# A state-space transform's last two pointwise operations on GpSimd, their input in two buffers, and kernel loads on SyncE's queue

## The chip, the cores and the metric

The kernel runs on one core of one Trainium2 chip. The time is the device time of one execution in microseconds (us), lower is better. The engines are named as in the profile: PE is TensorE's matmul, DVE is VectorE, ACT is ScalarE, POOL is GpSimd, and SP is SyncE, which here only issues DMAs.

## The reference

Two independent computations stand side by side in the output. Part A is a memory-augmented recurrent transformer, 64 segments one after the other. Part B is a long convolution of the S4 kind, and the change lies in it:

```python
P = jnp.exp(logdA[:, :, None] * l[None, None, :])
K = jnp.einsum('dn,dnl,dn->dl', Cc, P, dB).real
Kf = rfft2(pad(K)); Uf = rfft2(pad(u.transpose(0, 2, 1)))
Yf = Uf * Kf[None, :, :, :]
y = irfft2(Yf)[..., :L].transpose(0, 2, 1) + u * Dskip
return jnp.concatenate([a, b], axis=-1)
```

Here L is 2048, the model has 1024 channels, and all inputs and the output are bf16.

## The kernel before, in words

The program runs part B first, then part A. Part A needs weights that are loaded once (residents) and weights that are streamed again in each of the 64 segments.

Part B first builds the convolution kernel K and the spectra of u; K goes to DRAM as Kd, the spectra of u go there as Ud. What follows is the transform, from about 508 us of the profiled execution to 807 us. The channels are cut in two halves, dh=0 and dh=1, of 512 channels (DH). For each dh there are four frequency blocks kc, and each block is done in two half blocks, half=0 and half=1. One half block is one pass of the loop in `pointwise`:

- PE multiplies the kernel values KT with the cosine and sine matrix MF (L1137): 32 matmuls into two PSUM tiles s_[0] and s_[1]. There are three such PSUM buffers.
- ACT copies s_[1] into o_ (L1142, or L1144 and L1145).
- DVE adds and subtracts: X1 and X2 (L1150, L1151). Each reads s_[0] from PSUM and o_ from SBUF.
- DVE multiplies with the spectra of u: M1 to M4 (L1157 and L1158, twice each). They read uq and x, both in SBUF, in f32.
- DVE subtracts and adds in Y: Y1 and Y2 (L1159, L1160), both inputs in SBUF.
- DVE adds and subtracts the two halves of Y into Bt, as bf16 (L1163, twice): the last two operations of the half block.
- In dh=1, `inverses(2)` follows: two output blocks of dh=0 are made by 16 matmuls each (L1209), ACT scales the result into yb (L1214), DVE multiplies uu by Dskip and adds yb (L1215, L1216), and GpSimd issues the DMA that stores it (L1217).

Each engine runs its own instructions in program order, so an instruction that waits holds up all that follow on its engine. The same holds for the queues that issue DMAs. SP's queue in the transform holds, in this order for each frequency block: the loads mi and uu of the inverses (`load_inverse`, L1172 and L1174, three blocks ahead; uu has four buffers, freed when the store of a result has landed), and then the four loads uq of the next block's spectra (`load_u`, L963; four buffers, freed by M1 to M4). GpSimd's queue holds the 31 loads KT of the kernel values of dh=1 (`load_k`, L936, issued after the first block of dh=0), and the stores of the inverses. `load_k` for dh=0 runs earlier and on SP. The tile y has one buffer, x and o_ have one each.

After the eight half blocks of dh=1 come the remaining 16 inverses, those of dh=1, which read all of the second Bt. Beside each of them ACT issues two loads of part A's resident weights (L193). Then part A runs.

Of the kernel before, what the change touches and what calls it, by code (L numbers as in the profile page):

```python
# [10 lines left out]
BF16 = mybir.dt.bfloat16  # L11
F32 = mybir.dt.float32
# [584 lines left out]
def part_b(ctx, tc, u, A_re, A_im, B_re, B_im, C_re, C_im, log_dt, Dskip, out_b, ahead, copies, residents):  # L597
# [5 lines left out]
    DH, DQ = 512, 256  # L603
    v, sc, gp, pe, sy = nc.vector, nc.scalar, nc.gpsimd, nc.tensor, nc.sync
# [323 lines left out]
    def load_k(dh, qs, KT):  # L928
        dsl = slice(DH * dh, DH * dh + DH)

        def rows(r0, n, step=1):
            return Kd[r0:r0 + step * (n - 1) + 1:step, dsl]
        n_q = [0]

        def get(out, in_):
            qs[n_q[0] % len(qs)].dma_start(out=out, in_=in_)  # L936
            n_q[0] += 1
        for r in (0, 2, 1, 3):
            k0 = KT[:, 4 * r, :]
            get(k0[0:64], rows(r, 64, 4))  # L940
            get(k0[64:128], rows(256 + (0, 0, 1, 2)[r], 64, 2))
            k1 = KT[:, 4 * r + 1, :]
            if r == 2:
                get(k1[0:128:2], rows(384, 64, 2))
                get(k1[1:128:2], rows(386, 64, 2))
            else:
                get(k1[:], rows(384 + (0, 0, 0, 1)[r], 128))
            for mc in (2, 3):
                k2 = KT[:, 4 * r + mc, :]
                q0 = 512 + 64 * (mc - 2)  # L950
                get(k2[0:128:2], rows(q0, 64))
                if r == 0:
                    get(k2[1:128:4], rows(q0, 32, 2))
                    get(k2[3:128:4], rows(q0 + 2, 32, 2))
                else:
                    get(k2[1:128:2], rows(q0 + 1, 64))
        return KT

    def load_u(dh, kc):
        us = {}  # L960
        for q in (0, 2, 1, 3):
            us[q] = ahead.pool.tile([128, 2, 2, DQ], F32, name="uq", tag="wsl", bufs=4)
            sy.dma_start(out=us[q][:].rearrange("p a c d -> p a (c d)"), in_=Ud[kc, 2 * dh:2 * dh + 2, :, q].rearrange("a p c d -> p a (c d)"))  # L963
        return us
# [109 lines left out]
    for f in range(-1, 17):  # L1074
        if f == 15:
# [4 lines left out]
            ks = [load_k(0, (sy,), ahead.pool.tile([128, 16, DH], BF16, name="KT", tag="kst"))]  # L1080
# [32 lines left out]
    ktp = ctx2.enter_context(tc.tile_pool(name="b_KT", bufs=1))  # L1113
    bp0 = ctx2.enter_context(tc.tile_pool(name="b_B0", bufs=1))
    pw = ctx2.enter_context(tc.tile_pool(name="b_pw", bufs=1))
# [5 lines left out]
    def negate(KT):  # L1121
        KN = ahead.pool.tile([128, 8, DH], BF16, name="KN", tag="xTl")
        sc.activation(out=KN[:], in_=KT[:, 8:16, :], func=ACT.Copy, scale=-1.0)
        return KN

    def pointwise(dh, kc, KT, Bt):
        us = spectra.pop(0)
        for half in range(2):

            s_ = []  # L1130
            for r in range(2):
                ps = ps_h.tile([128, 2, DH], F32, name="hps", tag="h")
                for cs in range(2):
                    for i, rr in enumerate((r, r + 2)):
                        for mc in range(4):
                            rhs = KNs[dh][:, 4 * (rr - 2) + mc, :] if half == 1 and i == 1 else KT[:, 4 * rr + mc, :]
                            pe.matmul(ps[:, cs, :], lhsT=MF[:, 4 * rr + mc, cs, 128 * kc:128 * kc + 128], rhs=rhs,  # L1137
                                      start=(i == 0 and mc == 0), stop=(i == 1 and mc == 3))
                s_.append(ps)
            o_ = pw.tile([128, 2, DH], F32, name="osb_", tag="o")  # L1140
            if half == 0:
                sc.copy(out=o_[:], in_=s_[1][:])  # L1142
            else:
                sc.copy(out=o_[:, 0, :], in_=s_[1][:, 1, :])  # L1144
                sc.activation(out=o_[:, 1, :], in_=s_[1][:, 0, :], func=ACT.Copy, scale=-1.0)  # L1145
            if len(KNs) == dh:
                KNs.append(negate(KT))
            qs = (0, 2) if half == 0 else (3, 1)
            X = pw.tile([128, 2, 2, DH], F32, name="x", tag="x")
            v.tensor_tensor(out=X[:, 0], in0=s_[0][:], in1=o_[:], op=ALU.add)  # L1150
            v.tensor_tensor(out=X[:, 1], in0=s_[0][:], in1=o_[:], op=ALU.subtract)  # L1151
            Y = pw.tile([128, 2, 2, DH], F32, name="y", tag="y")
            split = "p c (a d) -> p c a d"
            for n_, q in enumerate(qs):
                uc, un = (us[q][:, :, i, :].unsqueeze(1).to_broadcast([128, 2, 2, DQ]) for i in range(2))
                x_ = X[:, n_].rearrange(split, a=2)
                v.tensor_tensor(out=Y[:, n_].rearrange(split, a=2), in0=uc, in1=x_, op=ALU.mult)  # L1157
                v.tensor_tensor(out=x_, in0=un, in1=x_, op=ALU.mult)  # L1158
            v.tensor_tensor(out=Y[:, :, 0, :], in0=Y[:, :, 0, :], in1=X[:, :, 1, :], op=ALU.subtract)  # L1159
            v.tensor_tensor(out=Y[:, :, 1, :], in0=Y[:, :, 1, :], in1=X[:, :, 0, :], op=ALU.add)  # L1160
            first = 0 if half == 0 else 1
            for j, op in ((0, ALU.add), (1, ALU.subtract)):
                v.tensor_tensor(out=Bt[:, kc, half, j], in0=Y[:, first], in1=Y[:, 1 - first], op=op)  # L1163
            inverses(2 if dh == 1 else 0)

    NIV = 3
# [1 line left out]
    def load_inverse(dh, c):  # L1168
        r, mc = c // 4, c % 4
        iv = ivs[-1]  # L1170
        mi = iv.tile([128, 2, 4, 128], BF16, name="mi", tag="mi", bufs=NIV)
        sy.dma_start(out=mi[:], in_=MId[c])  # L1172
        uu = iv.tile([128, 512], BF16, name="uu", tag="uu", bufs=NIV + 1)
        sy.dma_start(out=uu[:], in_=u_v[r, mc][:, DH * dh:DH * dh + DH])  # L1174
        return mi, uu
# [11 lines left out]
    def inverses(n):  # L1187

        for _ in range(n):
            dh_, c = todo.pop(0)  # L1190
            if not ready:
                ready.append(negated(c, nxt[0][0]))
            inverse(dh_, Bs[dh_], c, *nxt.pop(0), *ready.pop(0))
            if len(todo) >= NIV:
                nxt.append(load_inverse(*todo[NIV - 1]))
# [26 lines left out]
    for dh in range(2):  # L1222
        Bt = (bp0, bp)[dh].tile([128, 4, 2, 2, 2, DH], BF16, name="Bt", tag="B")
        Bs.append(Bt)
        if dh == 1:

            resident = residents()
            next(resident)
            todo = [(0, c) for c in range(16)] + [(1, c) for c in range(16)]
            nxt = [load_inverse(*todo[n_]) for n_ in range(NIV)]  # L1230
        for kc in range(4):
            pointwise(dh, kc, ks[dh], Bt)
            if kc < 3 or dh == 0:
                spectra.append(load_u(dh + (kc + 1) // 4, (kc + 1) % 4))
            if dh == 0 and kc == 0:
                ks.append(load_k(1, (gp,), ktp.tile([128, 16, DH], BF16, name="KT", tag="KT")))
    ctx2.close()
    ctx_m.close()
    for c in range(16):
# [4 lines left out]
def kernel(  # L1244
# [53 lines left out]
    with ExitStack() as ctx_b:  # L1298
        part_b(ctx_b, tc, B_u[0], B_A_re, B_A_im, B_B_re, B_B_im, B_C_re, B_C_im, B_log_dt, B_Dskip, out_b, ahead, copies, residents)
# [37 lines left out]
```

## Time and profile before

| what | us |
|---|---|
| median of 4 runs | 2485.24 |
| lowest and highest run | 2477.5, 2498.34 |
| the profiled execution's own time | 2477.5 |
| its span, first to last instruction | 2475.8 |
| L1163, one of the two last operations, on DVE, f32 to bf16, 1024 elements in each of 128 partitions | 1.22 |
| L1217, issue of a store on GpSimd | 0.54 |
| L936, issue of a KT load: on SP (median), on GpSimd (median) | 0.594, 0.542 |

The whole page's first lines give the shares over the span:

```profile
PE 2013.3 (81%) x32728; PEld 1082.0 (44%) x32774; DVE 1471.2 (59%) x3159; ACT 964.8 (39%) x1543; POOL 352.0 (14%) x629
PE   1689888866988688888888888888888888888879
DVE  9589788979881254545454545454545454545540
POOL 2235556540001100000000000000000000000020
DMA  6685964664349999999999999999999999999992
```

The first line gives each engine's busy time, its share of the span and its number of instructions. The others cut the span in 40 slices of 61.9 us; a digit is the busy share of a slice in tenths. The transform lies in slices 8 to 12, counted from 0. In slices 8 to 11 DVE has digits 7, 9, 8 and 8, GpSimd 4, 0, 0 and 0. A line of a timeline gives the start, the duration, engine, line, operation, output and inputs with their shapes, the number of instructions merged in it, and in brackets the idle time before it and what ended it. [...]

### The profile page before, as it was taken

The page shows a single profiled execution, that of the slowest core. Times are in us where ns is not written, and L with a number is a line of the kernel's source. Part 1 is how long each engine was busy: PE and PEld are TensorE (multiplying, and loading weights), DVE is VectorE, ACT ScalarE, POOL GpSimd, SP SyncE. Part 2 cuts the span into 40 slices and gives each one's busy share as a digit, 9 for nine tenths or more (in the row PEclk, how much of TensorE's full clock was granted, in tenths as well). Part 3 has the DMA queues.
Part 4 walks back from the last instruction along what each step waited for, and adds up shares of the span by engine and source line. Part 5 has one row for each costly group of instructions (what it writes and reads, how often), then busy time and mean ns, then how long its engine had stood idle before and what let it go on. Part 6 is the DMA issues. An engine that isn't in the chain of part 4 may idle for free.

```text
span 2475.8 us, 76297 instructions
## 1 busy us (share of the span) xinstructions
PE 2013.3 (81%) x32728; PEld 1082.0 (44%) x32774; DVE 1471.2 (59%) x3159; ACT 964.8 (39%) x1543; POOL 352.0 (14%) x629
## 2 busy tenths in 40 slices
PE   1689888866988688888888888888888888888879
PEld 1355565632433244444444444444444444444444
DVE  9589788979881254545454545454545454545540
ACT  6689788911212132323232333232333333333321
POOL 2235556540001100000000000000000000000020
PEclk9999999987989799999999999999999999999999
DMA  6685964664349999999999999999999999999992
GB/s 160 182 230 156 268 185 142 161 180 138 104 152 348 341 384 389 373 370 376 380 381 383 364 394 387 371 366 385 377 389 382 386 382 373 379 381 388 384 384 77
DMA packets 383273, 763.17 MB, mean 308 GB/s; under 512 B 119462, under 2 KB 211590, under 8 KB 380886
## 3 DMA queue, kind: packets, MB, share of 16 engines
q1 hardware_dynamic: 363094, 700.46, 78.4%
q0 software_dynamic: 14928, 39.99, 5.0%
q10 hardware_dynamic: 4912, 17.84, 2.0%
q8 instruction: 256, 4.19, 0.7%
q14 instruction: 83, 0.68, 0.1%
HBM read 703.35 MB, written 67.88 MB: 312 GB/s over the span
## 4 chain that ended last, share of the span: by engine, by line
DMA 32%; PE 29%; DVE 18%; issue 13%; ACT 6%; POOL 1%; SPq 1%; DVEq 0%; ACTq 0%; POOLq 0%
DMA wst<-WD_k 15%; PE acc L339 11%; DMA wst<-WD_o 9%; PE pp L438 3%; PE pe L561 2%; PE pro L158 2%; DVE nr L1026 2%; DMA wst<-WD_v 2%; PE ups L848 2%; PE tr L350 2%; DMA PVd<-vst 1%; DVE piece L278 1%; PE pa L995 1%; DMA wst<-WD_q 1%; DVE sc L385 1%
## 5 line engine op out<-in xcount | busy, mean ns | idle before, releaser
L339 PEld LDWEIGHTS <-hT 128*32 128x32 bf16 x12352 | 325.9, 96 | 466.2 <-issue 248.1
L339 PE MATMUL acc<-wst,hT 128*32 128x512 bf16 x3072 | 311.6, 390 | 161.3 <-DMA wst<-WD_k 66.0
L345 ACT CAST ev<-acc 128x512 bf16<-128x512 f32 x384 | 224.7, 585 | 406.0 <-PE acc L339 401.5
L438 PEld LDWEIGHTS <-oT 128*32 128x32 bf16 x8192 | 204.0, 97 | 111.5 <-issue 84.6
L278 DVE TENSOR_SCALAR piece<-keep 128x256 int32<-128x256 int32 (+1 forms) x640 | 191.5, 363 | 57.8 <-PE pp L438 31.2
L438 PE MATMUL pp<-W_o,oT 128*32 128x256 bf16 x5120 | 211.7, 276 | 8.1 <-DMA W_o<-in_A_Wo_dram 8.1
L339 PE MATMUL acc<-W_v,hT 128*32 128x512 bf16 x3072 | 210.9, 379 | 0.0
L377 DVE TENSOR_REDUCE mx<-sc 128x8 f32<-128x320 f32 x128 | 62.3, 487 | 243.4 <-PE sc L370 243.3
L339 PE MATMUL acc<-W,hT 128*32 128x512 bf16 x2560 | 204.4, 390 | 0.0
L351 DVE COPY KT<-tr 128x512 bf16<-128x512 bf16 x64 | 27.2, 425 | 261.8 <-PE tr L350 261.8
L438 PE MATMUL pp<-wst,oT 128*32 128x256 bf16 x2560 | 128.9, 278 | 33.4 <-DMA wst<-WD_o 24.3
L358 POOL COPY KT<-pk 128x128 bf16<-128x128 bf16 x128 | 37.7, 294 | 794.5 <-PE sc L370 447.3
L351 ACT COPY QT<-tr 128x512 bf16<-128x512 bf16 x128 | 74.9, 586 | 189.0 <-PE tr L350 189.0
L1209 PE MATMUL yp<-Bt,mi 128*128 128x512 bf16 x379 | 113.4, 405 | 35.1 <-DMA mi<-MId 27.3
L425 ACT CAST oT<-pv 128x512 bf16<-128x512 f32 x128 | 75.0, 586 | 170.4 <-PE pv L411 166.0
L339 PE MATMUL acc<-W_q,hT 128*32 128x512 bf16 x1792 | 134.2, 380 | 0.0
L312 POOL COPY hT<-xt 128x192 bf16<-128x192 bf16 x64 | 22.2, 347 | 729.5 <-DMA xt<-XTd 518.8
L158 PE MATMUL pro<-xTl,wsl 128*128 128x512 bf16 x493 | 120.7, 392 | 6.0 <-ACT xTl L102 5.2
L379 ACT ACTIVATE sc<-sc 128x320 f32<-128x320 f32 x128 | 54.0, 422 | 154.3 <-DVE sc L378 148.7
L339 PE MATMUL acc<-W_k,hT 128*32 128x512 bf16 x1536 | 107.3, 385 | 0.0
L1137 PE MATMUL hps<-KT,MF 128*128 128x512 bf16 x374 | 94.3, 397 | 15.9 <-DVE x L1151 14.9
L350 PE MATMUL tr<-a_ident,ev 128*128 128x128 bf16 x1024 | 101.7, 222 | 1.0 <-ACT KT L351 1.0
(280 smaller groups left out, 3627.0 us busy)
## 6 DMA issues: line engine op xcount, KB each, us to landing
wst<-WD_o SPq DMA_DIRECT2D x320, 512.0 KB
wst<-WD_k SPq DMA_DIRECT2D x256, 512.0 KB
wst<-WD_q SPq DMA_DIRECT2D x256, 512.0 KB
wst<-WD_v SPq DMA_DIRECT2D x256, 512.0 KB
Ud<-ux POOLq DMA_DIRECT2D x16, 1024.0 KB, 5.7
uq<-Ud SPq DMA_DIRECT2D x32, 512.0 KB
pk<-PKd SPq DMA_DIRECT2D x64, 192.0 KB
wsl<-in_A_Wk_dram SPq DMA_DIRECT2D x16, 512.0 KB
```

Of the source, the lines that this page charges most:

```text
L158: nc.tensor.matmul(a[:], lhsT=w[:, kc, 128 * j:128 * j + 128], rhs=xTl[:, kc, :, :].rearrange("p s k -> p (s k)"), start=(kc == 0), stop=( ...
L278: nc.vector.tensor_scalar(out=out.bitcast(I32), in0=in_.bitcast(I32), scalar1=0, scalar2=None, op0=ALU.bitwise_or)
L339: nc.tensor.matmul(a[32 * g:32 * g + 32, o_:o_ + rhs.shape[1]], lhsT=hT[:, kc, :], rhs=rhs, start=(kc == 0), stop=(kc == KC - 1), tile_pos ...
L345: nc.scalar.copy(out=q[:], in_=a[:])
L350: nc.tensor.transpose(out=p[:, i, hl, :, :].rearrange("p a b -> p (a b)"), in_=q[:, 128 * hl:128 * hl + 128], identity=ident[:])
L351: eng(out=dst, in_=p[:, i, :, :, :])
L377: nc.vector.tensor_reduce(out=mx[:], in_=sc, axis=AX.X, op=ALU.max)
L379: nc.scalar.activation(out=sc, in_=sc, func=ACT.Exp, scale=scale)
L425: nc.scalar.copy(out=o[:], in_=p[:].rearrange("p a (g q) -> p a g q", g=4))
L438: nc.tensor.matmul(po[32 * qt:32 * qt + 32, :], lhsT=oT[:, h % 4, (h % 16) // 4, :], rhs=columns(w, 1024 * hh + 256 * qt, 256)[0][1], star ...
L1137: pe.matmul(ps[:, cs, :], lhsT=MF[:, 4 * rr + mc, cs, 128 * kc:128 * kc + 128], rhs=rhs, start=(i == 0 and mc == 0), stop=(i == 1 and mc = ...
L1209: pe.matmul(yp[:], lhsT=m_[:, cs, kc, :], rhs=Bt[:, kc, half, j, c_, :], start=(n == 0), stop=(n == 15))
```

## The change

It has three parts, all in the transform of part B.

```diff
-            Y = pw.tile([128, 2, 2, DH], F32, name="y", tag="y")
+            Y = pw.tile([128, 2, 2, DH], F32, name="y", tag="y", bufs=2)
...
             first = 0 if half == 0 else 1
             for j, op in ((0, ALU.add), (1, ALU.subtract)):
-                v.tensor_tensor(out=Bt[:, kc, half, j], in0=Y[:, first], in1=Y[:, 1 - first], op=op)
+                (v if (dh, kc, half) == (1, 3, 1) else gp).tensor_tensor(out=Bt[:, kc, half, j], in0=Y[:, first], in1=Y[:, 1 - first], op=op)
...
             if dh == 0 and kc == 0:
-                ks.append(load_k(1, (gp,), ktp.tile([128, 16, DH], BF16, name="KT", tag="KT")))
+                ks.append(load_k(1, (sy,), ktp.tile([128, 16, DH], BF16, name="KT", tag="KT")))
```

The two operations that write Bt go from DVE to GpSimd in 15 of the 16 half blocks; in the very last one they stay on DVE. Their input y has two buffers instead of one. The 31 loads of the kernel values for dh=1 are issued by SP instead of GpSimd, at the same place in the program, so in SP's queue they stand behind the uq loads of block kc=1 and ahead of those of kc=2.

## The prediction

> **What bounds the kernel now.** I read the page first. Its second part puts the change, which touches only part B's transform, into slices 8 to 11 of 40; from slice 12 on the DMA engines are nine tenths busy. Next I asked for busy time in stretches: 518 to 614 us holds the eight half blocks of dh=0, 614 to 745 those of dh=1, and after that come the last inverses and part A.
>
> ```profile
> core 0: us, PE busy (x) PEld busy (x) DVE busy (x) ACT busy (x) POOL busy (x), PEclk, DMA share, GB/s
> 518.00:614.00 96.00, 62.57 (x247) 26.18 (x251) 93.92 (x81) 15.70 (x15) 19.30 (x36) 0.86 0.45 142
> 630.00:745.00 115.00, 102.97 (x449) 45.47 (x457) 94.57 (x102) 24.84 (x39) 8.59 (x16) 0.94 0.42 136
> 745.00:809.00 64.00, 51.32 (x211) 21.52 (x213) 11.19 (x28) 17.28 (x26) 10.16 (x34) 0.92 0.96 343
> 870.00:1000.00 130.00, 111.76 (x2308) 59.04 (x2300) 72.40 (x199) 42.01 (x82) 4.68 (x15) 1.00 1.02 386
> ```
>
> DVE is busy 93.9 of 96 us in dh=0, so DVE is the bound there. In dh=1 neither PE nor DVE is full. From 745 us the DMA share is 0.96 and more: weights stream in, and they start only when the transform ends. So what DVE gains or loses before its last Bt write moves the end of the kernel one for one. The view of waits for 620 to 745 us agrees: PE yp waits 7.3 us for DVE Bt.
>
> Then the DVE timeline, one half block of dh=0 (Y2, the two operations that move, X1 and X2 of the next half, its first multiplication M1):
>
> ```profile
> 551.08 1.22 DVE L1160 TENSOR_TENSOR y<-y,x 128x1024 f32<-128x1024 f32 x1
> 552.33 2.36 DVE L1163 TENSOR_TENSOR Bt<-y 128x1024 bf16<-128x1024 f32 x2
> 554.61 1.22 DVE L1150 TENSOR_TENSOR x<-hps,osb__7370 128x1024 f32<-128x1024 f32 x1
> 555.74 1.22 DVE L1151 TENSOR_TENSOR x<-hps,osb__7370 128x1024 f32<-128x1024 f32 x1
> 556.88 1.22 DVE L1157 TENSOR_TENSOR y<-uq,x 128x1024 f32<-128x1024 f32 x1
> ```
>
> One half runs from 542.77 to 554.61, 11.84 us, of which the pair takes 2.28 (552.33 to 554.61). In dh=1 the four short uu operations (U1 to U4) follow the pair, and at every second half DVE waits for uq:
>
> ```profile
> 639.38 1.22 DVE L1160 TENSOR_TENSOR y<-y,x 128x1024 f32<-128x1024 f32 x1
> 640.63 2.36 DVE L1163 TENSOR_TENSOR Bt<-y 128x1024 bf16<-128x1024 f32 x2
> 643.43 0.42 DVE L1216 TENSOR_TENSOR uu<-uu,yb 128x512 bf16<-128x512 bf16 x1
> 644.15 0.54 POOL L1217 DMA_DIRECT2D out_dram<-uu  x1 [15.84 <-DVE uu L1216]
> 646.25 0.33 SPq L1174 DMA_DIRECT2D uu<-in_B_u_dram  x1
> 646.63 3.30 SPq L963 DMA_DIRECT2D uq<-Ud  x4
> 652.23 1.23 DVE L1157 TENSOR_TENSOR y<-uq,x 128x1024 f32<-128x1024 f32 x1 [5.07 <-DMA uq<-Ud]
> ```
>
> The reader is to see a chain: U2 ends, GpSimd issues the output's DMA, its landing frees a uu buffer, SP (in order) loads uu and only then uq, and M1 starts 12.85 us after Y2 started.
>
> **What the Trainium skill says.** "SBUF — State Buffer", section "Who interferes with whom": VectorE and GpSimd share a port pair. A VectorE instruction with two SBUF inputs contends with a GpSimd instruction that reads SBUF, and the one that comes second "fully blocks" until the first is done; with at most one SBUF input, outside the two-port modes, it does not. The trace agrees wherever it can. These rows carry it:
>
> ```profile
> L864 POOL TENSOR_TENSOR ux<-us x16: 1262/1268/1277, 115.6 to 491.4; 128x512 f32<-128x512 f32 x16
> L867 POOL TENSOR_TENSOR ux<-us x64: 717/1222/1614, 118.1 to 496.9; 128x256 f32<-128x256 f32 x64
> L977 DVE TENSOR_TENSOR gi<-E,sn x32: 1106/1112/1647, 122.7 to 503.2; 128x1824 bf16<-128x1824 bf16 x32
> L860 DVE TENSOR_TENSOR us<-ua,ups x32: 675/680/682, 109.6 to 491.2; 128x512 f32<-128x512 f32 x32
> ```
>
> L860 reads one operand from PSUM; sixteen of its executions lie beside the GpSimd sum of L864, and neither stretches. L867 takes 0.72 us alone and up to 1.61 where VectorE runs L1026 and L1033 beside it. The one L977 that starts within an L867 (497.82) takes 1.65 instead of 1.11. That is one sighting for two SBUF inputs, in bf16; for f32 none.
> "GPSIMD Engine Reference", section "Performance versus the Vector engine", prices a two-input f32 sum of 2048 elements at 4497 ns, and the trace has 512 at 1268 ns. A line through both gives an estimate of 2.34 us for 1024; twice the 1.235 between two starts of L864 and L865 gives 2.47. I take 2.4.
>
> **The change part by part.** Call the moved pair P1 and P2, the multiplications M1 to M4, and s the start of Y2.
>
> (1) *The pair leaves DVE*: 15 of 16 halves, 2.28 us each. X1 and X2 read one operand from PSUM, so they run beside P1. M1 to M4, Y1, Y2 and U1 to U4 read two from SBUF and take turns with P1 and P2.
>
> (2) *A half of dh=0 after the change.* Y2 ends at s+1.22; GpSimd follows 0.1 later (L864 starts 0.08 to 0.2 after its DVE input), P1 from s+1.32 to s+3.72. X1 starts at s+1.14, M1 would start at s+3.41 and waits until 3.72. P2 is queued behind M1: M1 ends at 4.85, P2 at 7.25, and M2 waits for that. M2 to the next Y2 is 4.80 (546.28 to 551.08), so the next Y2 is at s+12.05 instead of 11.84: 0.2 worse. The first pair is hidden, since DVE waits there for ACT anyway (530.92, idle 0.68). Seven periods: +1.5 us. The gain is eaten almost exactly. Bounds of a period: -0.1 with P at 2.25, +0.5 with 2.55.
>
> (3) *An even half of dh=1.* U1 comes before P1 and holds to s+1.50; P1 to 3.90, U2 to 4.25, P2 to 6.65; only then U3, and 1.02 later X1 (643.78 to 644.80), at s+7.67. X1 to M1 is 2.27, M1 to Y2 6.05 (652.23 to 658.28): s+15.99, where before the step is 13.57 (658.28 to 671.85). +2.4. Here nothing free of the shared port lies beside P1 and P2.
>
> (4) *A half that waits for uq.* The output's DMA is behind P2 in GpSimd's queue and is issued at s+6.75, not s+4.77. Landing, uu, uq and M1 move with it: M1 at about s+14.85, while DVE is ready at s+9.94. +2.0.
> In dh=1 the first half absorbs its pair in the 3.59 us for which DVE waits for ACT (631.06), and the last stays on DVE. There remain three of each: 3*(2.4+2.0) = +13.2 us.
>
> (5) *Y in two buffers*: without it M1 of the next half would wait for P2. With it the buffer is free a half earlier; costs nothing.
>
> (6) *Kernel loads to SP.* The 31 KT DMAs leave GpSimd, where they ran from 526.9 to 547 and would have held P1 back. On SP they come after the uq of kc=1 (last at 538.09) and take about 21.5 us, as the first 31 did there (469.52). So the next uq goes out near 560 instead of 547.5 and is needed at 568.7: 8.7 us of room against 5.6 from issue to use above, so nothing lost; without this cover up to 3. KT is wanted at 592.5. "DMA: Bandwidth & Descriptors", section "Issuing engines are not separate DMA queues", says that the transfers run on the same 16 engines whoever issues, so I expect no speed from the move itself.
>
> Sum: 1.5+13.2, about +15 us. Against the profiled execution (2477.5 us, span 2475.8) that is 2492.5. The median of the runs shown is 7.7 higher, 2485.24, so I forecast 2500.
>
> **The rivals.**
> A, the forecast: whole instructions exclude each other. P between 2.25 and 2.55 gives +11 to +19, 2496 to 2504; the runs shown lie up to 13 us from their median, of which I allow 6 on either side: 2490 to 2510.
> B, partial: the f32 operations lose only about half of this, by waits that DVE has anyway. Between A and C: about -5 us, 2480. For it: DVE idles for uq in any case. Against it: that idle time lies after the pair, not beside it.
> C, the other side: f32 operations at one element per cycle leave the shared read path open. Then DVE gains 2.28 in seven halves (-16), gives back some 3 where uq(kc=2), issued at 560, is wanted at 561.9, and in dh=1 the output's DMA goes out 2.28 earlier: periods 16.6 and 11.3, sum 83.7 instead of 95.6 (639.38 to 734.94), -12. Together -25: 2460. For it: no f32 pair was seen side by side. Against it: L977, which reads through the same two inputs. It decides if M2 is not stretched. With a wait of w for each of P1 and P2, A's sum is about 7*(w-2.28)+3*(2w-2.4)+3*(2w-2.8) while P1 fits beside X1 and X2; it changes its sign at w = 1.7 us, below the lowest estimate of P.
> D, worse: SP's longer queue also costs uq transfers in dh=0, or a late output delays the mi loads and so PE: 10 to 20 more, about 2513.
>
> **How the numbers follow.** A 0.60, B 0.10, C 0.20, D 0.10. A measurement of this kernel tells about 0.5%, 12.4 us, from nothing; A straddles that bound, and some six tenths of it lie above. Slower: 0.37+0.10, rounded to 0.48; same: 0.23+0.10, less rounding 0.31; faster 0.21. The range 2474 to 2516 takes in A, B and most of D and leaves C out. A's own range is 2490 to 2510.
>
> **What would show it.** Steps 1 and 2: P rows of about 2.4 us on POOL and, in dh=0, X rows still 1.22 while M1 and M2 read above 1.22, the one or the other by some 2 us; the period near 12. Step 3: U2 and U3 near 2.5 us instead of 0.42. Step 4: the first output DMA of a half some 6.7 us after Y2 starts. Step 6: uq at about 560 with no DVE wait behind it. A period of 9.6 in dh=0 would prove me wrong, and so would Bt's last write before 735 us.

## The result and the profile after

| | before | after |
|---|---|---|
| median of the runs, us | 2488.65 (64 runs) | 2495.25 (43 runs) |
| lowest and highest, us | 2477.5, 2514.28 | 2480.72, 2512.33 |
| the profiled execution, us | 2477.5 | 2489.41 |
| its span, us | 2475.8 | 2487.7 |

The ratio after to before is 1.0026 with a 95% interval of 1.0015 to 1.0037. Taken times 2488.65 that is 6.5 us slower, between 3.7 and 9.2. Single runs scatter by more than that; only the many runs side by side show it.

First the stretches of the span that the prediction read, now for the kernel after:

```profile
core 0: us, PE busy (x) PEld busy (x) DVE busy (x) ACT busy (x) POOL busy (x), PEclk, DMA share, GB/s
518.00:614.00 96.00, 62.47 (x249) 26.21 (x254) 91.33 (x67) 15.08 (x14) 40.39 (x19) 0.85 0.44 145
630.00:745.00 115.00, 96.86 (x416) 42.44 (x424) 99.65 (x81) 23.20 (x36) 35.98 (x24) 0.92 0.38 125
745.00:809.00 64.00, 52.54 (x207) 21.83 (x210) 14.63 (x33) 15.54 (x23) 8.09 (x15) 0.88 0.89 314
```

From 518 to 614 us DVE ran 67 instructions instead of 81 and was still busy 91.33 us instead of 93.92. The 14 fewer would have freed 14 times 1.14 (half of the pair's 2.28), 16 us. So most of what left came back as longer rows: an instruction that waits for GpSimd in its row counts as busy. From 630 to 745 us DVE was *busier*, 99.65 against 94.57, with 21 instructions fewer. These two windows don't hold the same work, though: before, the last Bt write ended at 738.55, and after, the window closes before the last one.

The timeline shows where. Two halves of dh=0, one after the other, on DVE and GpSimd (a DVE row can start some 0.1 us before the row ahead of it ends, as 552.74 after 551.60 plus 1.23, so a period is taken from start to start):

```profile
538.57 1.22 DVE L1160 TENSOR_TENSOR y<-y,x 128x1024 f32<-128x1024 f32 x1
539.87 5.72 POOL L1163 TENSOR_TENSOR Bt<-y 128x1024 bf16<-128x1024 f32 x2 [7.74 <-DVE y L1160]
542.17 1.22 DVE L1157 TENSOR_TENSOR y<-uq,x 128x1024 f32<-128x1024 f32 x1
543.42 3.26 DVE L1158 TENSOR_TENSOR x<-uq,x 128x1024 f32<-128x1024 f32 x1
...
550.25 1.22 DVE L1160 TENSOR_TENSOR y<-y,x 128x1024 f32<-128x1024 f32 x1
551.54 4.65 POOL L1163 TENSOR_TENSOR Bt<-y 128x1024 bf16<-128x1024 f32 x2 [5.95 <-DVE y L1160]
551.60 1.23 DVE L1150 TENSOR_TENSOR x<-hps,osb__7370 128x1024 f32<-128x1024 f32 x1
552.74 1.22 DVE L1151 TENSOR_TENSOR x<-hps,osb__7370 128x1024 f32<-128x1024 f32 x1
553.87 3.41 DVE L1157 TENSOR_TENSOR y<-uq,x 128x1024 f32<-128x1024 f32 x1
557.31 1.23 DVE L1158 TENSOR_TENSOR x<-uq,x 128x1024 f32<-128x1024 f32 x1
...
562.11 1.22 DVE L1160 TENSOR_TENSOR y<-y,x 128x1024 f32<-128x1024 f32 x1
```

X1 and X2 (L1150, L1151), which read one operand from PSUM, keep their 1.22 us with GpSimd's pair beside them. A multiplication with both inputs in SBUF does not: in the first half M2 waits (3.26), in the second M1 (3.41). From Y2 to Y2 these halves take 11.68 and 11.86 us; before it was 11.84.

In dh=1, from the Y2 of a half that waits for uq:

```profile
638.61 1.22 DVE L1160 TENSOR_TENSOR y<-y,x 128x1024 f32<-128x1024 f32 x1
639.91 4.96 POOL L1163 TENSOR_TENSOR Bt<-y 128x1024 bf16<-128x1024 f32 x2 [10.81 <-DVE y L1160]
640.26 2.40 DVE L1216 TENSOR_TENSOR uu<-uu,yb 128x512 bf16<-128x512 bf16 x1
642.58 2.57 DVE L1215 TENSOR_TENSOR uu<-uu,Dsk 128x512 bf16<-128x512 bf16 x1
644.82 0.56 POOL L1217 DMA_DIRECT2D out_dram<-uu  x1
645.60 1.22 DVE L1150 TENSOR_TENSOR x<-hps,osb__7868 128x1024 f32<-128x1024 f32 x1
648.41 0.33 SPq L1174 DMA_DIRECT2D uu<-in_B_u_dram  x1
648.80 1.96 SPq L963 DMA_DIRECT2D uq<-Ud  x4
653.12 1.23 DVE L1157 TENSOR_TENSOR y<-uq,x 128x1024 f32<-128x1024 f32 x1 [5.18 <-DMA uq<-Ud]
```

U2 and U3 take 2.40 and 2.57 us instead of 0.42. The store, whose data U2 wrote by 642.66, is issued 2.2 us later, when GpSimd's pair has ended. M1 starts 14.51 us after Y2 (before: 12.85).

The view of waits from 620 to 745 us (engine, line, what it waited for: us in total, times, longest) gives DVE's largest:

```profile
DVE y L1157 <- DMA uq<-Ud: 13.1, 3, 5.2
```

It was 13.3 us, also three times. The longer halves did not use up this wait: it comes after the pair, and what ends it, the uq transfer, was itself made late.

The Y2-to-Y2 steps of dh=1, us, from the timelines. s0 is the first half of dh=1 and s7 the last; the last column runs from the first X1 to the end of the last write of Bt.

| | first X1 to s0 | s0 to s7 | the seven steps of dh=1 | to last Bt |
|---|---|---|---|---|
| before | 103.82 | 112.81 | 17.25, 18.90, 13.57, 17.56, 13.57, 18.03, 13.92 | 220.24 |
| after | 103.14 | 122.88 | 17.77, 20.58, 15.30, 19.37, 15.29, 19.29, 15.28 | 229.63 |

dh=0 gained 0.7 us and dh=1 lost 10.1, so the transform was 9.4 us longer in these two executions.

The first step of dh=1 is not set by the pair. X1 of its second half waits for ACT, ACT for PE's matmuls L1137, which come behind those of the inverses L1209 on PE, and these had waited for mi, the load of the first inverse. Before:

```profile
614.41 8.55 PE L1209 MATMUL yp<-Bt,mi 128*128 128x512 bf16 x31 [14.81 <-DMA mi<-MId]
631.06 1.23 DVE L1150 TENSOR_TENSOR x<-hps,osb__7757 128x1024 f32<-128x1024 f32 x1 [3.59 <-ACT osb__7757 L1145]
```

After:

```profile
630.29 1.23 DVE L1150 TENSOR_TENSOR x<-hps,osb__7757 128x1024 f32<-128x1024 f32 x1 [2.03 <-ACT osb__7757 L1145]
```

Counted from the transform's first X1 (518.31 and 517.70), this X1 stands at 112.75 before and at 112.59 after. So most of the 0.7 us that dh=0 gained is gone at this point, the step reads 0.5 longer because it starts earlier, and the pair of this half costs nothing.

### The profile page after: what moved, and what is told of

It reads as the page before. It is cut to its first block, busy times and chain, and to the rows that moved or that the text cites. A ratio compares the mean times of both kernels' runs of the same rounds, so it can differ in the third digit from the quotient of the medians.

```text
span 2487.7 us, 76294 instructions
## 1 busy us (share of the span) xinstructions
PE 2017.2 (81%) x32728; PEld 1080.5 (43%) x32774; DVE 1480.5 (60%) x3129; ACT 965.2 (39%) x1543; POOL 411.5 (17%) x628
## 4 chain that ended last, share of the span: by engine, by line
DMA 31%; PE 23%; DVE 8%; ACT 3%; issue 2%; SPq 1%; ACTq 0%; DVEq 0%
DMA wst<-WD_k 15%; PE acc L339 12%; DMA wst<-WD_o 10%; PE pp L438 3%; DMA wst<-WD_q 3%; DMA wst<-WD_v 2%; PE pe L561 2%; PE tr L350 2%; DVE piece L278 1%; ACT ev L345 1%; DMA W_o<-in_A_Wo_dram 1%; PE pv L411 1%; DVE ob L527 1%; DVE sc L378 1%; DVE sc L385 1%
## 5 line engine op out<-in xcount | busy, mean ns | idle before, releaser
L1209 PE MATMUL yp<-Bt,mi 128*128 128x512 bf16 x379 | 115.5, 411 | 43.2 <-DMA mi<-MId 33.1
L1137 PE MATMUL hps<-KT,MF 128*128 128x512 bf16 x374 | 95.3, 401 | 15.6 <-DVE x L1151 14.6
```

The costliest lines, as they stand in the source:

```text
L1209: pe.matmul(yp[:], lhsT=m_[:, cs, kc, :], rhs=Bt[:, kc, half, j, c_, :], start=(n == 0), stop=(n == 15))
```

## The experiments

The theory: a GpSimd instruction that reads SBUF and a DVE instruction with both inputs in SBUF take whole turns, which costs DVE about what it hands over (E, exclusion), and in dh=1 the store also stands behind the pair in GpSimd's queue (Q, queue). The rivals were that the loads moved to SP cost the time, and that the loss lies somewhere else, for instance in the traffic. Each kernel is given as a diff against the kernel after unless said otherwise.

**Only dh=0 moves its pair.**

```diff
-                (v if (dh, kc, half) == (1, 3, 1) else gp).tensor_tensor(...)
+                (v if dh == 1 else gp).tensor_tensor(...)
```

> The pair is on GpSimd in dh=0 alone; KT loads on SP and two Y buffers as in the change. Theory of whole-instruction exclusion: a half of dh=0 takes 11.7 to 11.85 us as in the changed kernel, so the stretch from the first X1 to the first Y2 of dh=1 stays near 103.1 us (103.8 before) and dh=1 is as before: within 2 us of the kernel before, ratio 0.999 to 1.001. Rival, that the loads moved to SP cost the time: about the changed kernel's loss, ratio 1.002 to 1.004. Rival, that a pair beside f32 work is a gain which dh=1 gives back: 8 us or more faster than before.

Measured: ratio 1.0000 (0.9981 to 1.0019). First X1 to s0 103.18 us, s0 to s7 113.52. dh=0 is 0.64 us shorter, not longer, and dh=1 within its scatter as before. X1 of the second half of dh=1 stands at 112.71 here, with DVE's pair in dh=1, so this gain, too, ends in the wait for PE.

**Only dh=1 moves its pair.**

```diff
-                (v if (dh, kc, half) == (1, 3, 1) else gp).tensor_tensor(...)
+                (v if dh == 0 or (kc, half) == (3, 1) else gp).tensor_tensor(...)
```

> The pair is on GpSimd in dh=1 alone (the last half excepted). Exclusion: the whole loss is here, some 9 us from the first Y2 of dh=1 to the last Bt write, ratio 1.002 to 1.004, U2 and U3 near 2.4 and 2.6 us as in the changed kernel. Rival, that the loads on SP cost it: no more loss than with the loads alone.

Measured: ratio 1.0026 (1.0008 to 1.0044), as much as the whole change. First X1 to s0 103.80, s0 to s7 123.04 us. So the loss sits in dh=1. The same X1 stands at 112.85.

**Loads and buffers only.**

```diff
-                (v if (dh, kc, half) == (1, 3, 1) else gp).tensor_tensor(...)
+                v.tensor_tensor(...)
```

> The pair stays on DVE everywhere; only the KT loads are on SP and Y has two buffers. Exclusion: nothing, ratio 0.999 to 1.001, no DVE wait for uq in dh=0. Rival, that the longer SP queue delays uq of kc=2: DVE waits up to 3 us there and the ratio is about 1.001; rival, that the loads on SP are the loss: 1.002 to 1.004.

Measured: ratio 1.0009 (0.9989 to 1.003); 103.83 and 114.12 us. No cost is seen, though the interval allows some 7 us. The steps tell more: dh=0 is as before, and in dh=1 the 1.3 us more lie in the three halves that wait for uq (19.74, 17.76, 18.30 against 18.90, 17.56, 18.03), with the even halves at 13.57 as before.

The five executions of these kernels (s0 to s7 112.81, 113.52, 114.12 us with the pair of dh=1 on DVE; 122.88, 123.04 with it on GpSimd) give the scatter of dh=1 and the size of its loss: mean 113.48 against 122.96, 9.5 us. In dh=0 the three with the pair on DVE have 103.80 to 103.83, the two with it on GpSimd 103.14 and 103.18.

**Extra sums on GpSimd, whose result nobody reads.** The pair is back on DVE, by the same line as in `loads_only`. If the loss came from waiting for GpSimd's result, this would cost little; if it is exclusion, it costs in full.

```diff
+            Z = pw.tile([128, 2, DH], BF16, name="z", tag="z")
+            for _ in range(2):
+                gp.tensor_tensor(out=Z[:], in0=Y[:, 0], in1=Y[:, 1], op=ALU.add)
             inverses(2 if dh == 1 else 0)
```

> As the kernel with the loads alone, plus two more sums on GpSimd in every half block, of the same size and inputs as the pair (Y into a tile that nothing reads), while the pair itself stays on DVE. Exclusion: in dh=0 one of them runs beside X1 and X2 and the other holds DVE for its 2.3 us, so a half takes about 14.1 us instead of 11.84; in dh=1 both hold DVE, so an even half takes about 18 us instead of 13.6. Rival, that GpSimd's work only shares the path or only costs where something waits for its result: nothing waits here, so 11.84 and 13.6 stay, within 0.3.

Measured: 2532.52 in one run, 45.4 us above the median of the kernel before beside it (2487.09). First X1 to s0 120.24, s0 to s7 138.94. Its timeline, dh=0:

```profile
553.70 4.51 DVE L1163 TENSOR_TENSOR Bt<-y 128x1024 bf16<-128x1024 f32 x2
553.81 6.61 POOL L1166 TENSOR_TENSOR z<-y 128x1024 bf16<-128x1024 f32 x2 [7.38 <-DVE y L1160]
558.13 1.21 DVE L1150 TENSOR_TENSOR x<-hps,osb__7379 128x1024 f32<-128x1024 f32 x1
```

DVE's own pair takes 4.51 us instead of 2.36, GpSimd's two sums 6.61 instead of 4.65, because they take turns. A half of dh=0 is 13.99 us, 2.15 more than before, and an even half of dh=1 17.88 to 18.21, where about 18 were expected. In dh=0 this is the exclusion with nothing else that delays DVE. The last Bt write comes 44.7 us later than before; that the one run's time agrees to the microsecond is in part luck, since single runs scatter by more.

**Extra writes on GpSimd.** The same place, the pair again on DVE, but GpSimd is kept busy by two memsets, which read nothing. An 8-element copy ahead of them makes them start after Y2.

```diff
+            Z = pw.tile([128, 2048], BF16, name="z", tag="z")
+            gp.tensor_copy(out=Z[:, 0:8], in_=Y[:, 1, 1, DH - 8:DH])
+            for _ in range(2):
+                gp.memset(Z[:], 0.0)
             inverses(2 if dh == 1 else 0)
```

> As the kernel with two extra sums, but GpSimd only writes: after a copy of eight elements of Y, which makes it wait for Y2, two memsets of 2048 bf16 each[...]. If it is the second read of DVE's two-input operations that GpSimd holds up, and not GpSimd's being busy or its writes, then a half of dh=0 stays at 11.84 us, within 0.3, and an even half of dh=1 at 13.6 to 14. Rival, that anything on GpSimd that uses the shared path holds DVE: about 2 us more a half.

Measured: 2489.27 in one run; 103.80 and 118.66 us. The seven steps of dh=1: 17.73, 21.43, 13.56, 19.04, 13.57, 19.41, 13.92. From its timeline, a half of dh=0 and then one of dh=1:

```profile
553.87 2.36 DVE L1163 TENSOR_TENSOR Bt<-y 128x1024 bf16<-128x1024 f32 x2
553.97 1.17 POOL L1165 CAST z<-y 128x8 bf16<-128x8 f32 x1 [6.94 <-DVE y L1160]
555.21 3.67 POOL L1167 MEMSET z<- 128x2048 bf16 x2
558.42 1.21 DVE L1157 TENSOR_TENSOR y<-uq,x 128x1024 f32<-128x1024 f32 x1
...
641.37 1.22 DVE L1160 TENSOR_TENSOR y<-y,x 128x1024 f32<-128x1024 f32 x1
643.96 3.67 POOL L1167 MEMSET z<- 128x2048 bf16 x2
645.42 0.43 DVE L1220 TENSOR_TENSOR uu<-uu,yb 128x512 bf16<-128x512 bf16 x1
647.58 1.07 POOL L1221 DMA_DIRECT2D out_dram<-uu  x2
```

Here the two causes come apart. GpSimd is busy for about as long as with the pair, but DVE's rows keep their length, M1 (558.42) and U2 (645.42) beside a memset too, and the even halves take their 13.56 to 13.92. The halves that wait for uq are nevertheless 1.4 to 2.5 us longer, since the store goes out at Y2 plus 6.21 us, exactly where it went with the pair, though U2 had ended at Y2 plus 4.48. So Q costs without E, in the odd halves (those that wait for uq) alone; the even halves are E.

**The uq loads ahead of the inverses' loads, on the kernel before.** DVE waits 13.3 us for uq; this asks whether that wait is a transfer or only SP's order. `load_u` of the next block moves from the block loop to a point ahead of the inverses of the second half:

```diff
+            if half == 1 and (kc < 3 or dh == 0):
+                spectra.append(load_u(dh + (kc + 1) // 4, (kc + 1) % 4))
             inverses(2 if dh == 1 else 0)
...
-            if kc < 3 or dh == 0:
-                spectra.append(load_u(dh + (kc + 1) // 4, (kc + 1) % 4))
```

> The kernel before, with one move: in dh=1 SP issues the uq loads of the next block ahead of the four loads of the inverses, not behind them. If the 13.3 us for which DVE waits for uq in dh=1 are a matter of SP's order, they go; then a half takes about 13.8 us, PE's time for 64 matmuls, and the stretch from the first to the last Y2 of dh=1 falls from 112.8 to about 100 us: ratio 0.994 to 0.996. Rival, that the uq transfers are slow whatever their place: no change.

Measured: ratio 0.993 (0.9908 to 0.9951), 17 us faster and a little more than expected; s0 to s7 is 100.29 us, and the last Bt write comes 12.6 us earlier than before, which lies inside the 12 to 23 us of the interval. The stretch 630 to 720 us, with the columns of the first fence, and the waiting half's timeline:

```profile
630.00:720.00 90.00, 89.53 (x409) 40.81 (x417) 85.63 (x89) 23.38 (x37) 6.46 (x12) 1.00 0.47 146
```

```profile
629.39 9.32 SPq L963 DMA_DIRECT2D uq<-Ud  x4
639.50 1.22 DVE L1160 TENSOR_TENSOR y<-y,x 128x1024 f32<-128x1024 f32 x1
646.37 0.33 SPq L1176 DMA_DIRECT2D uu<-in_B_u_dram  x1
647.19 1.21 DVE L1157 TENSOR_TENSOR y<-uq,x 128x1024 f32<-128x1024 f32 x1
```

All four uq loads are issued by 638.71, before Y2, and M1 starts 7.69 us after Y2 without a wait. After the first, 17.39, all halves now take 13.74 to 13.91, close to the 13.57 and 13.92 that the halves without a wait had before: DVE goes from one instruction to the next, and PE is busy 89.53 of the 90 us, so that the next limit is close. The wait was SP's order, not a slow transfer.

**The same on the kernel after.**

> The changed kernel with the same move of the uq loads. Theory: the loss in dh=1 has two parts, GpSimd's turns on the shared path (even halves, 15.3 us instead of 13.6) and the store of a result queued behind the pair on GpSimd, which moves the uq loads (odd halves). With the uq loads freed from the store, all halves of dh=1 take 15.3 us: from the first to the last Y2 some 109.5 us instead of 122.9, still 1.5 us a half behind the kernel with the early loads and the pair on DVE. Rival, that DVE hides the pair where it no longer waits for uq: the same time as that kernel.

Measured: ratio 0.9963 (0.9947 to 0.9979). s0 to s7 is 109.56 us: 17.82 and then six steps of 15.29. With Q out of the way the pair still costs 9.3 us in dh=1 (109.56 against 100.29), 8.8 of it in these six steps, now through E:

```profile
660.31 2.39 DVE L1218 TENSOR_TENSOR uu<-uu,yb 128x512 bf16<-128x512 bf16 x1
662.62 2.57 DVE L1217 TENSOR_TENSOR uu<-uu,Dsk 128x512 bf16<-128x512 bf16 x1
665.64 1.22 DVE L1150 TENSOR_TENSOR x<-hps,osb__7972 128x1024 f32<-128x1024 f32 x1
667.91 1.21 DVE L1157 TENSOR_TENSOR y<-uq,x 128x1024 f32<-128x1024 f32 x1
```

**One operation on GpSimd, beside X1 and X2 only.** If one GpSimd operation of 2.35 us just fits beside X1 and X2 (2.27), and the other one stays on DVE but is issued after X2, nothing is left to exclude. In dh=1 both stay on DVE:

```diff
+            if kept_B:
+                kept_B.pop(0)(v)
             Y = pw.tile([128, 2, 2, DH], F32, name="y", tag="y", bufs=2)
...
+                if dh == 1:
+                    put_B(v)
+                elif j == 0:
+                    put_B(gp)
+                else:
+                    kept_B.append(put_B)
```

`put_B` is the operation of L1163 on the engine that it is given.

> Only in dh=0, and only one operation of the pair on GpSimd, the other on DVE behind X1 and X2 of the next half; dh=1 as before; loads on SP as in the change. Exclusion: GpSimd's operation now lies wholly beside X1 and X2, which read one operand from PSUM, so DVE gains one operation a half: a half of dh=0 takes 10.8 to 10.9 us instead of 11.84, the stretch from the first X1 to the first Y2 of dh=1 97 us instead of 103.8, ratio 0.997 to 0.998. Rival, that GpSimd also holds X1 and X2: 11.7 us or more a half.

Measured: ratio 0.9967 (0.9948 to 0.9986). Halves of dh=0 take 10.77 and 10.80 us, after a first one of 13.76; first X1 to s0 is 97.57. The timeline, from one Y2 to the next:

```profile
551.22 1.22 DVE L1164 TENSOR_TENSOR y<-y,x 128x1024 f32<-128x1024 f32 x1
552.51 2.35 POOL L1168 TENSOR_TENSOR Bt<-y 128x1024 bf16<-128x1024 f32 x1 [8.41 <-DVE y L1164]
552.57 1.23 DVE L1152 TENSOR_TENSOR x<-hps,osb__7369 128x1024 f32<-128x1024 f32 x1
554.84 1.22 DVE L1168 TENSOR_TENSOR Bt<-y 128x1024 bf16<-128x1024 f32 x1
555.97 1.22 DVE L1161 TENSOR_TENSOR y<-uq,x 128x1024 f32<-128x1024 f32 x1
562.02 1.22 DVE L1164 TENSOR_TENSOR y<-y,x 128x1024 f32<-128x1024 f32 x1
```

No row is stretched, and the half is 1.06 us shorter, nearly the whole of one operation (1.14). The same offload that gains nothing as a pair gains as a single one. The first half loses 1.15, because there the pair had lain in a wait for ACT. dh=0 is 6.3 us shorter, but the first step of dh=1 is 19.52 instead of 17.25: DVE waits longer for ACT there (5.87 against 3.59), and so 2.3 us of the gain go. The last Bt write came 3.9 us earlier; the medians give 8.2, 3.5 to 12.9.

**Both, `one_beside_x` with the early uq loads.**

> The early uq loads together with one operation of the pair on GpSimd beside X1 and X2 in dh=0; in dh=1 the pair is on DVE. If the two gains are of different stretches they add: about 97 us from the first X1 to the first Y2 of dh=1, about 100 us from there to the last Y2, ratio 0.989 to 0.992 to the kernel before. Rival, that the second gain is hidden by PE or by the weights that follow: no better than the early loads alone, 0.993.

Measured: ratio 0.9921 (0.989 to 0.9953), 20 us faster than the kernel before and so faster than both kernels of the case. First X1 to s0 97.57, s0 to s7 102.25, the last Bt write 16.8 us earlier than before. The traces put it 4.2 us ahead of the early loads alone, with a first step of 19.34 against 17.39; so the two gains add only in part. The intervals of the times overlap (0.9908 to 0.9951 for the early loads alone), so the times alone don't rule out the rival that the second gain is hidden.

## Why the prediction was right in kind and too large in size

The direction of the whole, the two mechanisms and their places were as the prediction put them; in dh=0 a small gain came in place of a small loss. Its sum of 14.7 us was measured at 9.4 in the two executions of before and after (from all executions without and with: -0.7 + 9.5 = 8.8), and at 6.5, 3.7 to 9.2, between the medians. The 8.8 lie inside that interval, so the traces and the medians don't contradict each other; how much of the remaining 2 us is scatter and how much is taken back after the transform the runs don't settle. The largest share of the chance, 0.48, was put on slower by over 0.5%; what came, 0.26%, had been given 0.31. That the forecast of 2500 lies within 5 us of 2495.25 is in part luck: it started from a median of 2485.24, and with 64 runs the median of before is 3.4 higher. From there the sum would have led to 2503.

- *Step 1*, what runs beside P1: right. X rows stayed at 1.21 to 1.23, M rows were stretched. P was taken as 2.4 us; one alone is 2.35 (`one_beside_x`, 552.51), two back to back 4.65. "GPSIMD Engine Reference", section "Performance versus the Vector engine", had led to the estimate of 2.34, on the line through its 4497 ns and the trace's 1268, which was the better of the two estimates. "SBUF — State Buffer", section "Who interferes with whom", says that the port pair which the two engines share is an exclusive lock; for f32 the extra sums show it, 4.51 instead of 2.36 us.
- *Step 2*, +1.5 us for dh=0: came out as -0.7. The half is 11.68 or 11.86 instead of 12.05. Where M2 waits, the order was the one assumed (P1, M1, P2, M2), but the pair ended at s+7.02 (545.59), not 7.25, since P was shorter, and the next multiplication began 1.01 after that (546.60), where M2 had been booked with a full 1.15. We call this distance the restart; after a wait it was shorter than between two undisturbed rows. Where M1 waits for both, an order the step did not foresee, M2 starts at s+7.06 (557.31), and the rest is as booked.
- *Step 3*, even half +2.4: measured +1.73, +1.72 and +1.36. X1 starts at s+6.99, not 7.67. The pair ends at s+6.26 instead of 6.65: 0.15 from P, and 0.22 because U1 and U2 together lengthened the pair by 0.31 (4.96 against 4.65), not by the 0.53 that the step gave them. The other 0.29 is U3: X1 follows the pair's end by 0.73, not 1.02, a shorter restart, as in step 2. Again the right event with a size read from an undisturbed row.
- *Step 4*, half that waits for uq +2.0: measured +1.68, +1.81, +1.26. The store went out at s+6.21, predicted 6.75, for the reasons of step 3, and M1 started at s+14.51, predicted 14.85. Between them the step had simply moved the rest along; in fact the uu load came 3.59 us after the store (before 2.10) and M1 4.32 after the first uq issue (before 5.60). Why the two changed against each other was not pursued. The extra memsets show that the queue alone makes this half late.
- *First half of dh=1*, predicted to absorb its pair: right. DVE still waits 2.03 us for ACT there, and the X1 after it is not late (112.59 against 112.75). The step is 0.52 longer (17.77 against 17.25) because dh=0 ended earlier, so it takes back most of the 0.7 of step 2.
- *Steps 5 and 6*, nothing: right as far as `loads_only` can tell (1.0009, 0.9989 to 1.003); what Y's second buffer alone does was not tried. The uq of kc=2 went out at 557.57, and M1 at 565.70 did not wait.

In the sum: dh=0 with the first half of dh=1 was 1.7 too high (1.5 against -0.7 + 0.5), even halves 2.4, odd halves 1.3. 14.7 - 1.7 - 2.4 - 1.3 = 9.3.

The rivals: C (no exclusion) falls with M1 at 3.41 and with the extra sums. Its own sum had a slip: it let the store go out 2.28 us earlier, though its pair would still have stood ahead of the store on GpSimd, which by itself makes the store 1.44 later (6.21 against 4.77 after Y2, `extra_memsets`). It also took 16.6 for all three halves that wait for uq, which fits only the longest (18.90 - 2.28). B (half of the gain kept) falls with `dh0_only` at 1.0000 and no shorter dh=1. D (SP's queue) falls with `loads_only`; its other half, a PE made late by mi, costs nothing here, since DVE's waits in dh=1 after the change are 13.1 us for uq, 2.0 for the ACT of the first step and 0.5 within DVE. A holds with a smaller P and a shorter restart.

## What to carry to other kernels

In this kernel, an operation that reads SBUF and went from DVE to GpSimd gained only what fitted beside DVE instructions that read at most one operand from SBUF, or into a wait that DVE had anyway. So count that window first, and move no more than fills it (here one operation of 2.35 us beside X1 and X2, 1.06 us gained a half, where two gained next to nothing). If GpSimd also issues DMAs, an operation put ahead of an issue can delay it and all that its landing frees. And a wait for a transfer that stands behind another wait in an in-order DMA queue may be only an order: moving the four uq loads ahead of the four loads of the inverses was worth 17 us, more than the whole question of the engines.

## What was not expected of the hardware

- The turns are not always taken in the same order. In dh=0 the pair takes 5.72 us in the second half of each block, with M1 between its two instructions, and 4.65 in the first half, where GpSimd runs both without a break. The cost to DVE is nearly the same (11.68 and 11.86). M1's row starts 2.30 us after the pair's in the one (539.87, 542.17) and 2.33 in the other (551.54, 553.87), both times about when the first sum of 2.35 ends. So it is a near tie; what decides it was not tried.
- GpSimd waits for DVE as well. Its copy of 8 elements a partition beside DVE's pair takes 1.17 us where it starts 0.10 after the pair (553.97 after 553.87), 1.09 where it starts 0.19 after (529.60) and 0.87 where it starts 0.40 after (613.46). Each time it ends 1.27 or 1.28 us after the pair's start, when the first of DVE's two instructions (1.22) has just ended. So most of its time is a wait for its turn.
